# A forgetting-attention and SwiGLU kernel: loading q and k as eight rows per partition and moving the reordering to other reads of PSUM

## The chip, the cores and the metric

The kernel runs on one core of a Trainium2 chip. A core has a matrix engine (PE, in the profile also PEld for its weight loads), a vector engine (DVE), a scalar engine (ACT), a third elementwise engine (POOL) that does not touch PSUM in this kernel, and a queue engine (SP) that issues transfers; ACT and POOL issue a few transfers too. The metric is the device time of one execution in microseconds (us). Durations of single instructions are given in nanoseconds (ns).

## What is computed

There are 8 batches of 8 heads, 576 positions and a head size of 64. Each query row is scored against the keys up to its own position; a forget gate adds a decay that is a difference of cumulated log gates; a softmax and the weighted values follow. The result, 4608 tokens of 512 features, goes through a gated feed-forward block with 1536 hidden features.

```python
scores = scale * np.matmul(q, k.transpose(0, 1, 3, 2))
cum = np.cumsum(np.log(np.clip(f, 0.0001, 1.0)), axis=-1)
scores = np.where(causal, -1000000000.0, scores + cum[:, :, :, None] - cum[:, :, None, :])
attn = softmax(scores); x = np.matmul(attn, v)          # x: 4608 tokens x 512
g = x @ w_gate
out = (g * sigmoid(g) * (x @ w_val)) @ w_out
```

## The kernel before

The unit of the attention is a pair: two heads of one batch, 32 pairs in all (NPAIR). The 576 positions are cut into 9 blocks of 64 (QB), and a score tile holds 64 queries of one head in partitions 0 to 63 and the same 64 queries of the other head in partitions 64 to 127. The 9 query blocks of a pair are split into two groups, g=0 with blocks 0 to 3 and g=1 with blocks 4 to 8.

For one pair the steps are these. `load_pair` (L320) brings k and q in as float32, each with one transfer for both heads. Partition p holds a few consecutive rows: for k 96 partitions of 6 rows, for q 72 partitions of 8 rows (ROWS, L182). `prepare` (L337) casts them to bf16 (kb at L352, qb at L350, nearly always on POOL, on ACT at L348 for one pair of the start), transposes them on PE (L364) into a PSUM tile tx, 6 transposes of 96 columns for k and 8 of 72 for q, and copies tx to SBUF. The j-th transpose holds the rows j, j+6, j+12 and so on, so positions lie in tx in a permuted order. The copy (L380 on DVE, L378 on ACT) puts them back: it writes its target in natural order and reads PSUM with a step of 96 bf16 elements for k (tile kt, one copy for the pair) or 72 for q (tile qz, one copy for each head).

`scores` (L387) multiplies qz by kt into a PSUM tile sp (L399) and adds a causal mask to the last 64 columns of each query block with a second, 64-column matmul of the identity by the mask (L403). DVE then adds the gates' cumulated sum from cb, writes t, and keeps the running minimum (L415, a custom instruction); ACT takes the exponential (L429). `normalize` divides (L464 on POOL) into bf16 tiles pk. These are transposed, for the first 8 pairs on PE (L488, with copies at L493), for the others by a transposing transfer (L476), into pT. `weighted` (L496) multiplies by the values into xo, in the PSUM pool tx (L514), and `spread` (L521) copies the result into the ring xT (L538, ACT or DVE), the input of the feed-forward part. There `gate` makes two products (L595), tanh on ACT (L601, tile th, three buffers) and two DVE steps (L603, L606), and `project` (L609) makes the output product (L620), a copy and a transfer.

The order of everything is computed when the kernel is built. A planner (`Plan.order`, L54) holds for every step the engines that may do it with a cost for each, its dependencies, the buffer pools, and a priority; it always starts the step that can start first, ties by priority, and thereby also chooses the engine where several are allowed. Each engine then executes its own list in order. So a step's assumed cost, such as 600 on ACT and 680 on DVE for the copies of L378 and L380, decides both where it runs and what stands before and behind it. Feed-forward steps fill PE wherever attention steps cannot go; after the last attention step the rest of the feed-forward work follows.

Of the kernel before, what the change touches and what calls it, by code (L numbers as in the profile page):

```python
# [157 lines left out]
def kernel(  # L158
# [20 lines left out]
    NPAIR = B * NPB  # L179
    KD = DM // P  # L180
    KF = DF // P
    ROWS = {"k": (96, 6), "q": (72, 8)}  # L182
    scale = 1.0 / (D ** 0.5)
    assert NB * QB == S and D == 64 and all(a * b == S for a, b in ROWS.values())

    TILES = [256, 256] + [512] * 7 + [256, 256]
    NRING = 2560
# [34 lines left out]


    ident = sb.tile([P, P], BF16)
    maskf = sb.tile([P, QB], F32)
    mask = sb.tile([P, QB], BF16)
    xT = sb.tile([P, KD, NRING], BF16)
# [2 lines left out]
    wo = sb.tile([P, KF, DM], BF16)  # L230


    bufs("qf", [P, 2, ROWS["q"][1] * D], F32, 2)
    bufs("kf", [P, 2, ROWS["k"][1] * D], F32, 2)
    bufs("qb", [P, ROWS["q"][1], 2, D], BF16, 2)
    bufs("kb", [P, ROWS["k"][1], 2, D], BF16, 2)
    bufs("kt", [P, S], BF16, 5)
    bufs("qz", [P, NB, 2, QB], BF16, 5)
    bufs("cb", [P, S], F32, 5)
# [80 lines left out]
    def load_pair(p):  # L320
        b, hp = divmod(p, NPB)
        s = first[p]
        for name, src, pr in (("k", k, 0), ("q", q, .1)):
            pl.key((name + "f", p), name + "f")
            loads[name, p] = pl.op({"SP": 620} if p else {"ACT": 620}, lambda e, name=name, src=src: (nc.scalar if e == "ACT" else nc.sync).dma_start(
                out=pl.buf((name + "f", p))[0:ROWS[name][0], :, :],
                in_=src[b, 2 * hp:2 * hp + 2].rearrange("h (p r) d -> p h (r d)", r=ROWS[name][1])),
                (), [(name + "f", p)], (-99 + 3 * p if p < NPB else s) + pr, dma=1130 if name == "k" else 980, after=[sums[p - 3, 0 if p - 3 >= NPB else 1]] if p >= NPB else [])
        if p >= NDIRECT:
            pl.key(("cb", p), "cb")  # L330
            for h in range(2):
                loads["cb", p, h] = pl.op({"SP": 600}, lambda e, h=h: nc.sync.dma_start(
                    out=pl.buf(("cb", p))[64 * h:64 * h + 64, :],
                    in_=cum_dram[2 * p + h:2 * p + h + 1, :].to_broadcast((64, S))),
                    ["cum_dram"], [("cb", p), (("cb", p), 3)], -98.5 + 3 * p if p < NPB else s + .2, dma=560)

    def prepare(p):  # L337
        s = first[p]
        for name in ("k", "q"):
            fk, bk = (name + "f", p), (name + "b", p)  # L340
            KR, KC = ROWS[name]
            pl.key(bk, name + "b")

            def cast(e, name=name, fk=fk, bk=bk, KR=KR):
                src = pl.buf(fk)[0:KR, :, :].rearrange("p h (r d) -> p r h d", d=D)
                dst = pl.buf(bk)[0:KR, :, :, :]
                if e == "ACT":
                    nc.scalar.activation(dst, src, AF.Copy, scale=-scale if name == "q" else 1.0)  # L348
                elif name == "q":
                    eng[e].tensor_scalar(dst, src, -scale, 1.0, op0=ALU.mult, op1=ALU.mult)  # L350
                else:
                    eng[e].tensor_copy(dst, src)  # L352
            engs = {"POOL": 850}
            if p < NPB:
                engs = {"POOL": 850, "ACT": 850, "DVE": 500} if name == "k" else {"POOL": 1050, "ACT": 1050, "DVE": 680}
# [5 lines left out]
            def transpose(e, bk=bk, tk=tk, KR=KR, KC=KC):  # L361
                src = pl.buf(bk).rearrange("p r h d -> p r (h d)")
                for j in range(KC):
                    nc.tensor.transpose(half(tk)[:, KR * j:KR * j + KR], src[0:KR, j, :], ident[0:KR, 0:KR])  # L364
            pl.op({"PE": KC * (KR / 2.4 + 2.5)}, transpose, [bk], [tk], s - 1, lat=200)
            halves = [(0, P, None)] if name == "k" else [(0, 64, 0), (64, 128, 1)]
            ok = ("kt", p) if name == "k" else ("qz", p)
            pl.key(ok, ok[0])
            for a, z, h in halves:
                def evac(e, a=a, z=z, h=h, tk=tk, ok=ok, KC=KC):  # L370
                    if h is None:
                        src = half(tk)[a:z, 0:S].rearrange("r (j p) -> r p j", j=KC)
                        dst = pl.buf(ok)[a:z, :].rearrange("r (p j) -> r p j", j=KC)
                    else:
                        src = half(tk)[a:z, 0:S].rearrange("r (j i p) -> r i p j", j=KC, i=NB)
                        dst = pl.buf(ok)[a:z, :, h, :].rearrange("r i (p j) -> r i p j", j=KC)
                    if e == "ACT":
                        nc.scalar.copy(dst, src)  # L378
                    else:
                        nc.vector.tensor_copy(dst, src)  # L380
                pl.op({"ACT": 600, "DVE": 680}, evac, [tk] + ([("z", "qz", p)] if h is not None and p < 5 else []), [ok], s - .9)

    def epool(i):
        return f"e{i}" if i % 2 == 0 else "eo"
# [1 line left out]
    def scores(p, g):  # L386
# [3 lines left out]
        for n, bank in enumerate(BANKS[g]):  # L390
# [4 lines left out]
            def mult(e, bank=bank, sk=sk):  # L395
                sp, kt, qz, o = pl.buf(sk), pl.buf(("kt", p)), pl.buf(("qz", p)), 0
                for i, a, z in bank:
                    last = z == QB * (i + 1)
                    nc.tensor.matmul(sp[:, o:o + z - a], qz[:, i, :, :].rearrange("p h r -> p (h r)"), kt[:, a:z],  # L399
                                     start=True, stop=not last)  # L400
                    o += z - a
                    if last:
                        nc.tensor.matmul(sp[:, o - QB:o], ident, mask, start=False, stop=True)  # L403
            cols = [z - a for _, a, z in bank] + [64 for i, a, z in bank if z == QB * (i + 1)]
            pl.op({"PE": mm(*cols)}, mult, [("kt", p), ("qz", p), "mask"], [sk], pr, lat=220)
            o = 0
            for i, a, z in bank:
                last = z == QB * (i + 1)
# [4 lines left out]
                def add(e, i=i, a=a, z=z, o=o, sk=sk, tk=tk, last=last):  # L413
                    tm = pl.buf(("tm", p, g))
                    nc.vector.tensor_tensor_reduce(  # L415
                        out=pl.buf(tk)[:, a:z], in0=pl.buf(sk)[:, o:o + z - a], in1=pl.buf(("cb", p))[:, a:z], scale=1.0,
                        scalar=HUGE if a == 0 else tm[:, NB:NB + 1], op0=ALU.add, op1=ALU.min,
                        accum_out=tm[:, i:i + 1] if last else tm[:, NB:NB + 1])
                w = [tk, ("tm", p, g)] + ([("m", p, i)] if last else [("m", p, i, "part")])
# [101 lines left out]
    def spread(p, g):  # L521
# [5 lines left out]
        for a, z in ((0, cut), (cut, w)):  # L527
            if a == z:
                continue

            def evac(e, a=a, z=z):
                x0 = (t0 + a * QB) % NRING
                dst = xT[:, hp, x0:x0 + QB * (z - a)].rearrange("p (i r) -> p i r", r=QB)
                x = w - z
                src = pl.buf(xk)[:, QB * x:QB * (x + z - a)].rearrange("p (i r) -> p i r", r=QB)
# [183 lines left out]
```

## Time and profile before

| | |
|---|---|
| median of 3 runs | 437.74 us (436.67 to 437.89) |
| profiled execution | 437.73 us |
| its span, first to last instruction | 436.0 us |
| what lies around the span | 1.73 us |
| granted PE clock | 1.000 |
| busy PE / DVE / ACT / POOL | 402.5 / 347.9 / 302.8 / 252.1 us |
| instructions of PE / DVE / ACT / POOL | 3192 / 1081 / 848 / 452 |

All durations come from the profiled execution. The page lists busy time by engine, the span in 40 slices, the transfer queues, a chain of waits followed back from the last instruction, and the costliest groups of instructions. A group names its line, engine, operation, "output<-inputs", shapes and count, then busy time and mean, then the idle time of its engine before it and what ended that. PE's matmuls overlap in the pipeline: the duration of one (for example 379 ns for 512 columns) is its latency, and the distance between starts is what it occupies. "DMA share" can exceed 1 because transfers in flight overlap.

### The profile page before, as it was taken

The numbers are of one execution on the slowest core, as the hardware profiler recorded it, in microseconds if no ns is written. First come the engines' busy times: TensorE is split into PE (matmuls) and PEld (weight loads), VectorE is DVE, ScalarE is ACT, GpSimd is POOL, SyncE is SP. The second block draws the span as 40 slices with busy tenths as digits, with TensorE's granted clock in tenths as the row PEclk, the third lists the DMA queues.
The fourth block names the chain that finished last, engine by engine and source line by source line (L and its number), as shares of the span: only waits on it lengthen the run. The fifth ranks groups of instructions, "written<-read, shape, count | busy, mean of one in ns | idle before, by whom it ended". The sixth has DMA issues, their size and how long they took to land.

```text
span 436.0 us, 9859 instructions
## 1 busy us (share of the span) xinstructions
PE 402.5 (92%) x3192; PEld 229.2 (53%) x3192; DVE 347.9 (80%) x1081; ACT 302.8 (69%) x848; POOL 252.1 (58%) x452
## 2 busy tenths in 40 slices
PE   2578999998999998989999999999999999999996
PEld 1436777755454454444555554555445444457662
DVE  6788799798999798977999998999989665365340
ACT  6799789989877968776798777677678633232321
POOL 5699748748956855886668768938875600000000
PEclk9999999999999999999999999999999999999999
DMA  7999999637978998999999999999994640010112
GB/s 195 212 188 227 203 207 215 165 101 212 192 169 187 225 215 188 194 218 234 198 207 213 222 219 206 189 223 207 202 199 100 117 108 26 24 50 24 50 50 72
DMA packets 143956, 72.51 MB, mean 166 GB/s; under 512 B 118560, under 2 KB 130592, under 8 KB 143904
## 3 DMA queue, kind: packets, MB, share of 16 engines
q1 hardware_dynamic: 137732, 66.57, 71.9%
q0 software_dynamic: 5808, 4.72, 7.1%
q10 hardware_dynamic: 364, 0.59, 0.6%
q8 instruction: 25, 0.41, 0.4%
q14 instruction: 27, 0.22, 0.2%
HBM read 47.33 MB, written 9.58 MB: 131 GB/s over the span
## 4 chain that ended last, share of the span: by engine, by line
PE 60%; DVE 12%; DMA 10%; ACT 9%; POOL 4%; issue 4%; SPq 1%; DVEq 0%; ACTq 0%; POOLq 0%
PE gv L595 29%; PE op L620 15%; DMA qf<-in_q_dram 7%; PE sp L399 5%; DVE t L415 4%; PE tx L514 4%; ACT eo L429 3%; ACT e L429 2%; PE tx L364 2%; DVE qz L380 2%; DVE th L603 2%; POOL pk L464 2%; DMA pT<-pk 2%; PE gv L620 2%; DVE hh L606 2%
## 5 line engine op out<-in xcount | busy, mean ns | idle before, releaser
L415 DVE CUSTOM_DVE_ANT_0 t<-sp,cb 128x512 f32<-128x512 f32 (+7 forms) x288 | 130.4, 476 | 12.2 <-PE sp L403 5.9
L464 POOL TENSOR_SCALAR pk<-e,lr 128x512 bf16<-128x512 f32 (+3 forms) x186 | 97.7, 529 | 33.3 <-DVE tm L415 17.6
L595 PE MATMUL gv<-xT,wv 128*128 128x512 bf16 (+1 forms) x528 | 111.2, 340 | 0.2 <-DVE th L603 0.2
L595 PE MATMUL gv<-xT,wg 128*128 128x512 bf16 (+1 forms) x528 | 111.2, 340 | 0.2
L601 ACT ACTIVATE th<-gv 128x512 f32<-128x512 f32 x108 | 64.1, 594 | 61.0 <-PE gv L595 59.7
L603 DVE SCALAR_TENSOR_TENSOR th<-th,gv 128x512 f32<-128x512 f32 x108 | 73.9, 684 | 37.5 <-ACT th L601 37.1
L429 ACT ACTIVATE e<-t,tm 128x448 f32<-128x448 f32 (+4 forms) x160 | 88.8, 556 | 20.2 <-DVE tm L415 19.6
L620 PE MATMUL op<-wo,hh 128*128 128x512 bf16 x396 | 100.7, 379 | 2.1 <-DVE ot L632 1.3
L606 DVE TENSOR_TENSOR hh<-th,gv 128x512 bf16<-128x512 f32 x108 | 73.4, 685 | 10.3 <-PE op L620 4.1
L399 PE MATMUL sp<-kt,qz 128*128 128x448 bf16 (+4 forms) x320 | 72.3, 294 | 9.2 <-DVE tm L415 8.1
L429 ACT ACTIVATE eo<-t,tm 128x256 f32<-128x256 f32 (+3 forms) x128 | 71.2, 556 | 6.4 <-DVE tm L415 6.0
L595 PEld LDWEIGHTS <-wg 128*128 128x128 bf16 x528 | 48.9, 98 | 37.1 <-issue 0.2
L464 POOL TENSOR_SCALAR pk<-eo,lr 128x128 bf16<-128x128 f32 (+3 forms) x123 | 65.3, 531 | 2.5 <-ACT th L601 1.0
L595 PEld LDWEIGHTS <-wv 128*128 128x128 bf16 x528 | 47.8, 98 | 34.9 <-issue 0.3
L620 PEld LDWEIGHTS <-hh 128*128 128x128 bf16 x432 | 39.6, 98 | 41.8 <-issue 2.3
L403 PE MATMUL sp<-mask,ident 128*128 128x64 bf16 x288 | 48.1, 197 | 0.0
L399 PEld LDWEIGHTS <-qz 128*128 128x128 bf16 x320 | 30.6, 100 | 24.5 <-DVE qz L380 2.7
L350 POOL TENSOR_SCALAR qb<-qf 72x1024 bf16<-72x1024 f32 x31 | 32.9, 1062 | 14.8 <-DMA qf<-in_q_dram 7.2
L352 POOL CAST kb<-kf 96x768 bf16<-96x768 f32 x31 | 25.4, 820 | 27.4 <-DMA kf<-in_k_dram 19.3
L403 PEld LDWEIGHTS <-ident 128*128 128x128 bf16 x288 | 27.0, 100 | 21.3 <-issue 11.0
L557 POOL CAST vt<-vf 128x512 bf16<-128x512 f32 (+1 forms) x40 | 24.3, 608 | 17.4 <-DMA vf<-in_v_dram 17.2
L514 PE MATMUL tx<-pT,vt 128*64 128x320 bf16 (+4 forms) x448 | 29.7, 266 | 1.5 <-ACT e L429 0.5
(61 smaller groups left out, 393.2 us busy)
## 6 DMA issues: line engine op xcount, KB each, us to landing
out_dram<-ot SPq DMA_DIRECT2D x35, 256.0 KB, 2.4
kf<-in_k_dram SPq DMA_DIRECT2D x31, 288.0 KB, 6.3
qf<-in_q_dram SPq DMA_DIRECT2D x31, 288.0 KB
cb<-cum_f SPq DMA_DIRECT2D x62, 144.0 KB, 4.7
vf<-in_v_dram SPq DMA_DIRECT2D x32, 256.0 KB, 4.4
wo<-in_moe_w_out_dram POOLq DMA_DIRECT2D x3, 512.0 KB, 9.9
vf<-in_v_dram SPq DMA_DIRECT2D x8, 128.0 KB
wg<-in_moe_w_gate_dram POOLq DMA_DIRECT2D x2, 512.0 KB, 9.1
```

Source lines behind the costliest of these rows:

```text
L350: eng[e].tensor_scalar(dst, src, -scale, 1.0, op0=ALU.mult, op1=ALU.mult)
L399: nc.tensor.matmul(sp[:, o:o + z - a], qz[:, i, :, :].rearrange("p h r -> p (h r)"), kt[:, a:z], start=True, stop=not last)
L403: nc.tensor.matmul(sp[:, o - QB:o], ident, mask, start=False, stop=True)
L415: nc.vector.tensor_tensor_reduce(out=pl.buf(tk)[:, a:z], in0=pl.buf(sk)[:, o:o + z - a], in1=pl.buf(("cb", p))[:, a:z], scale=1.0, scalar= ...
L429: nc.scalar.activation(pl.buf(ek)[:, :L], pl.buf(tk)[:, :L], AF.Exp, bias=pl.buf(("tm", p, g))[:, i:i + 1], scale=-1.0, accum_out=pl.buf(( ...
L464: eng[e].tensor_scalar(dst, src, r, 1.0, op0=ALU.mult, op1=ALU.mult)
L514: nc.tensor.matmul(xo[r, 0:QB * n], vt[:, c, 2 * hp + h, :], pT[:, a:a + n, 64 * h:64 * h + 64], start=(c == 0), stop=(c == nch - 1))
L595: nc.tensor.matmul(pl.buf(bk)[:, j * n:j * n + n], wt[:, ko, fc * P:fc * P + P], xT[:, ko, x0:x0 + n], start=ko == 0, stop=ko == KD - 1)
L601: pl.op({"ACT": 487}, lambda e, u=u: nc.scalar.activation(pl.buf(("th", t, u)), pl.buf(("wg", t, u)), AF.Tanh, scale=0.5), [("wg", t, u)], ...
L603: pl.op({"DVE": 605}, lambda e, u=u: nc.vector.scalar_tensor_tensor(pl.buf(("th", t, u)), pl.buf(("th", t, u)), 1.0, pl.buf(("wg", t, u)), ...
L606: pl.op({"DVE": 605}, lambda e, u=u: nc.vector.tensor_mul(pl.buf(("hh", t, u)), pl.buf(("th", t, u)), pl.buf(("wv", t, u))), [("u", t, u), ...
L620: nc.tensor.matmul(pl.buf(bk), hh[:, (fc % nf) * n + ms * P:(fc % nf) * n + ms * P + P], wo[:, fc, :], start=fc == 0, stop=fc == KF - 1)
```

## The change

Both q and k now come in as 72 partitions of 8 rows (R = 8, PR = 72), so k has 8 transposes of 72 columns. The copies from PSUM no longer put anything in order for k: the copy of kt is a plain copy of 576 elements. For q the copy writes block by block, 64 columns a block, and reads PSUM in runs of 8 elements. Keys and queries therefore stay in a permuted order, and it is undone in two later places that read PSUM anyway. The score matmul reads kt in 8 runs of one eighth of its columns; the gate step reads sp with a step (an eighth of the matmul's columns, in float32) and writes t in natural key order. The queries stay permuted within each block of 64 until `spread`, whose copy reads the PSUM tile with a step of 8 within a block. The mask is made for that order of queries, and its matmul uses a permuted identity, perm, as the stationary operand and writes its 64 columns as 8 runs of 8. POOL makes perm once at the start. The planner's costs change: kb may cost 1050 instead of 850, a copy on DVE 380 instead of 680, and the transfer of q 1130 instead of 980. The tile th gets two buffers instead of three.

```diff
-    ROWS = {"k": (96, 6), "q": (72, 8)}
+    R = 8
+    PR = S // R
...
-    bufs("th", [P, 512], F32, 3)
+    bufs("th", [P, 512], F32, 2)
...
-            compare_op=ALU.is_ge, fill=BIG, base=0, pattern=[[-1, QB]], channel_multiplier=1,
+            compare_op=ALU.is_ge, fill=BIG, base=0, pattern=[[-1, R], [-R, R]], channel_multiplier=1,
...
+    setup({"POOL": 250}, lambda e: nc.gpsimd.tensor_copy(perm.rearrange("k (h j p) -> k h j p", h=2, j=R),
+                                                         ident.rearrange("k (h p j) -> k h j p", h=2, j=R)), ["perm"], -149)
...
-                out=pl.buf((name + "f", p))[0:ROWS[name][0], :, :],
-                in_=src[b, 2 * hp:2 * hp + 2].rearrange("h (p r) d -> p h (r d)", r=ROWS[name][1])),
+                out=pl.buf((name + "f", p))[0:PR, :, :],
+                in_=src[b, 2 * hp:2 * hp + 2].rearrange("h (p r) d -> p h (r d)", r=R)),
...
-            engs = {"POOL": 850}
+            engs = {"POOL": 1050}
...
-                for j in range(KC):
-                    nc.tensor.transpose(half(tk)[:, KR * j:KR * j + KR], src[0:KR, j, :], ident[0:KR, 0:KR])
+                for j in range(R):
+                    nc.tensor.transpose(half(tk)[:, PR * j:PR * j + PR], src[0:PR, j, :], ident[0:PR, 0:PR])
...
+                    src = half(tk)[a:z, 0:S]
                     if h is None:
-                        src = half(tk)[a:z, 0:S].rearrange("r (j p) -> r p j", j=KC)
-                        dst = pl.buf(ok)[a:z, :].rearrange("r (p j) -> r p j", j=KC)
+                        dst = pl.buf(ok)[a:z, :]
                     else:
-                        src = half(tk)[a:z, 0:S].rearrange("r (j i p) -> r i p j", j=KC, i=NB)
-                        dst = pl.buf(ok)[a:z, :, h, :].rearrange("r i (p j) -> r i p j", j=KC)
+                        src = src.rearrange("r (j i p) -> r i j p", j=R, p=R)
+                        dst = pl.buf(ok)[a:z, :, h, :].rearrange("r i (j p) -> r i j p", j=R)
...
-                pl.op({"ACT": 600, "DVE": 680}, evac, ...
+                pl.op({"ACT": 600, "DVE": 380}, evac, ...
...
-                    nc.tensor.matmul(sp[:, o:o + z - a], qz[:, i, :, :].rearrange("p h r -> p (h r)"), kt[:, a:z],
-                                     start=True, stop=not last)
+                    to = sp[:, o:o + z - a].rearrange("r (j p) -> r j p", j=R)
+                    nc.tensor.matmul(to, qz[:, i, :, :].rearrange("p h r -> p (h r)"),
+                                     kt.rearrange("d (j p) -> d j p", j=R)[:, :, a // R:z // R], start=True, stop=not last)
...
-                        nc.tensor.matmul(sp[:, o - QB:o], ident, mask, start=False, stop=True)
+                        nc.tensor.matmul(to[:, :, (z - a - QB) // R:], perm, mask.rearrange("r (j p) -> r j p", j=R),
+                                         start=False, stop=True)
...
-                        out=pl.buf(tk)[:, a:z], in0=pl.buf(sk)[:, o:o + z - a], in1=pl.buf(("cb", p))[:, a:z], scale=1.0,
+                        out=pl.buf(tk)[:, a:z].rearrange("r (p j) -> r p j", j=R),
+                        in0=pl.buf(sk)[:, o:o + z - a].rearrange("r (j p) -> r p j", j=R),
+                        in1=pl.buf(("cb", p))[:, a:z].rearrange("r (p j) -> r p j", j=R), scale=1.0,
...
-                src = bass.AP(src.tensor, src.offset + QB * (z - a - 1), [full[0], [-QB, z - a], full[2]])
+                src = bass.AP(src.tensor, src.offset + QB * (z - a - 1), [full[0], [-QB, z - a], [1, R], [R, R]])
```

More of the change, by code (lines that the diff above doesn't have):

```diff
@@ L181 @@
     KF = DF // P
-    ROWS = {"k": (96, 6), "q": (72, 8)}
+    R = 8
+    PR = S // R
     scale = 1.0 / (D ** 0.5)
-    assert NB * QB == S and D == 64 and all(a * b == S for a, b in ROWS.values())
+    assert NB * QB == S and D == 64 and R * R == QB
     TILES = [256, 256] + [512] * 7 + [256, 256]
@@ L224 @@
     ident = sb.tile([P, P], BF16)
+    perm = sb.tile([P, P], BF16)
     maskf = sb.tile([P, QB], F32)
@@ L230 @@
     wo = sb.tile([P, KF, DM], BF16)
[L233 to L236, printed above, removed]
+    bufs("qf", [P, 2, R * D], F32, 2)
+    bufs("kf", [P, 2, R * D], F32, 2)
+    bufs("qb", [P, R, 2, D], BF16, 2)
+    bufs("kb", [P, R, 2, D], BF16, 2)
     bufs("kt", [P, S], BF16, 5)
@@ L325, in load_pair @@
             loads[name, p] = pl.op({"SP": 620} if p else {"ACT": 620}, lambda e, name=name, src=src: (nc.scalar if e == "ACT" else nc.sync).dma_start(
[L326 to L328 removed]
+                out=pl.buf((name + "f", p))[0:PR, :, :],
+                in_=src[b, 2 * hp:2 * hp + 2].rearrange("h (p r) d -> p h (r d)", r=R)),
+                (), [(name + "f", p)], (-99 + 3 * p if p < NPB else s) + pr, dma=1130, after=[sums[p - 3, 0 if p - 3 >= NPB else 1]] if p >= NPB else [])
         if p >= NDIRECT:
@@ L352, in cast @@
                     eng[e].tensor_copy(dst, src)
-            engs = {"POOL": 850}
+            engs = {"POOL": 1050}
             if p < NPB:
-                engs = {"POOL": 850, "ACT": 850, "DVE": 500} if name == "k" else {"POOL": 1050, "ACT": 1050, "DVE": 680}
+                engs = {"POOL": 1050, "ACT": 1050, "DVE": 680}
             o = pl.op(engs, cast, [fk], [bk], s - 1 + (name == "q") * .1)
@@ L380, in evac @@
                         nc.vector.tensor_copy(dst, src)
-                pl.op({"ACT": 600, "DVE": 680}, evac, [tk] + ([("z", "qz", p)] if h is not None and p < 5 else []), [ok], s - .9)
+                pl.op({"ACT": 600, "DVE": 380}, evac, [tk] + ([("z", "qz", p)] if h is not None and p < 5 else []), [ok], s - .9)
     def epool(i):
@@ L398, in mult @@
                     last = z == QB * (i + 1)
-                    nc.tensor.matmul(sp[:, o:o + z - a], qz[:, i, :, :].rearrange("p h r -> p (h r)"), kt[:, a:z],
-                                     start=True, stop=not last)
+                    to = sp[:, o:o + z - a].rearrange("r (j p) -> r j p", j=R)
+                    nc.tensor.matmul(to, qz[:, i, :, :].rearrange("p h r -> p (h r)"),
+                                     kt.rearrange("d (j p) -> d j p", j=R)[:, :, a // R:z // R], start=True, stop=not last)
                     o += z - a
                     if last:
-                        nc.tensor.matmul(sp[:, o - QB:o], ident, mask, start=False, stop=True)
+                        nc.tensor.matmul(to[:, :, (z - a - QB) // R:], perm, mask.rearrange("r (j p) -> r j p", j=R),
+                                         start=False, stop=True)
             cols = [z - a for _, a, z in bank] + [64 for i, a, z in bank if z == QB * (i + 1)]
-            pl.op({"PE": mm(*cols)}, mult, [("kt", p), ("qz", p), "mask"], [sk], pr, lat=220)
+            pl.op({"PE": mm(*cols)}, mult, [("kt", p), ("qz", p), "mask", "perm"], [sk], pr, lat=220)
             o = 0
```

17 lines of the change are left out of this document (8 added, 9 removed).

## The prediction

> **What bounds the kernel now.** I read the page's busy times first, then busy time by stage, then the chain of waits, then the groups with shapes kept apart.
>
> ```profile
> PE 402.5 (92%) x3192; PEld 229.2 (53%) x3192; DVE 347.9 (80%) x1081; ACT 302.8 (69%) x848; POOL 252.1 (58%) x452
> ```
>
> By stage (start-up, attention with feed-forward filling, feed-forward alone):
>
> ```profile
> core 0: us, PE busy (x) PEld busy (x) DVE busy (x) ACT busy (x) POOL busy (x), PEclk, DMA share, GB/s
> 0.00:40.00 40.00, 22.51 (x213) 15.31 (x214) 31.49 (x114) 32.56 (x93) 30.86 (x71) 1.00 1.01 206
> 40.00:340.00 300.00, 288.16 (x2436) 162.75 (x2434) 271.29 (x890) 239.81 (x698) 216.17 (x372) 1.00 0.96 196
> 340.00:436.00 96.00, 91.83 (x547) 51.09 (x545) 45.09 (x79) 30.40 (x60) 5.11 (x10) 1.00 0.21 57
> ```
>
> PE is nearly full from 40 us on, and DVE is at 90% in the attention stage. A busy PE counts latencies, so I measured what a matmul occupies from the starts in the timeline:
>
> ```profile
> 205.74 0.28 PE L399 MATMUL sp<-kt,qz 128*128 128x256 bf16 x1
> 205.86 0.19 PE L403 MATMUL sp<-mask,ident 128*128 128x64 bf16 x1
> 205.89 0.25 PE L399 MATMUL sp<-kt,qz 128*128 128x192 bf16 x1
> ...
> 207.01 0.42 PE L364 MATMUL tx<-ident,kb 96*128 96x96 bf16 x6
> 207.26 0.42 PE L364 MATMUL tx<-ident,qb 72*128 72x72 bf16 x8
> 207.52 1.03 PE L595 MATMUL gv<-xT,wv 128*128 128x512 bf16 x4
> ```
>
> 256 columns take 0.12 us, 64 take 0.03, six transposes of 96 take 0.25 and eight of 72 take 0.26: columns / 2.4 + 2.5 ns, the same rule that gives 216 ns for 512 columns. Summed over all starts, PE has 379 us of such work. In the 432 us from the span's start to the end of the last matmul it lies empty 4.8 us before the first one, 22.2 us in the rest of the first 40, 25.6 us from 40 to 340 and 0.5 us later. Those 48 us between matmuls are all that a change without PE work in it can win. The chain says who owns them:
>
> ```profile
> PE 60%; DVE 12%; DMA 10%; ACT 9%; POOL 4%; issue 4%; SPq 1%; DVEq 0%; ACTq 0%; POOLq 0%
> PE gv L595 29%; PE op L620 15%; DMA qf<-in_q_dram 7%; PE sp L399 5%; DVE t L415 4%; PE tx L514 4%; ACT eo L429 3%; ACT e L429 2%; PE tx L364 2%; DVE qz L380 2%; DVE th L603 2%; POOL pk L464 2%; DMA pT<-pk 2%; PE gv L620 2%; DVE hh L606 2%
> ```
>
> The reader is to see DVE as second, with the copy of qz, which the change touches, among its lines.
>
> **Copies out of PSUM, on DVE.** These rows decide:
>
> ```profile
> L380 DVE COPY qz<-tx 64x576 bf16<-64x576 bf16 x36 | 27.2, 754 | 4.1 <-PE tx L364 1.8 <-ACT qz L378 1.5
> L380 DVE COPY kt<-tx 128x576 bf16<-128x576 bf16 x20 | 15.0, 752 | 2.0 <-PE tx L364 1.8
> L378 ACT COPY kt<-tx 128x576 bf16<-128x576 bf16 x12 | 7.6, 633 | 3.7 <-PE tx L364 3.7
> ...
> L493 DVE COPY pT<-gv 128x1024 bf16<-128x1024 bf16 x6 | 4.1, 688 | 1.0 <-PE gv L488 0.8
> L493 DVE COPY pT<-gv 128x384 bf16<-128x384 bf16 x4 | 1.4, 349 | 0.4 <-PE gv L488 0.4
> ```
>
> L493 copies bf16 from PSUM without a step at (688 - 349) / 640 = 0.53 ns per element, so 576 elements without a step cost 349 + 192 x 0.53 = 451 ns. With a step they cost 752 to 754, 1.04 ns per element. For kt I take 451. For qz, in runs of 8, the trace has no row: between 451 and 754; I take 451, since its neighbours in a run adjoin as in L493. ACT gains nothing: its row at 1024 elements is 1009 and at 384 it is 485, which gives 642 for 576, beside 633 measured with the step.
>
> The order of instructions shows 19 + 44 such copies on DVE (20 + 36 before), so DVE has 63 x 0.451 = 28.4 us instead of 42.2: 13.8 less. A few other copies move to it (+1.5), so 12.3 us less. ACT has 33 of them instead of 40 and a little less besides: 5.5 us less.
>
> What of it is on the path: adding up the chain's pieces, 12 of qz (8.9 us) and 4 of kt (2.8) stand in it on DVE. One such place:
>
> ```profile
> 45.74 0.44 PE tx L364 x6
> 46.21 0.77 DVE kt L380
> ```
>
> 40% of those 11.7 us is **4.7 us**. The lower bound is 2.7: kt's 1.2, and 0.125 for each of 12 qz pieces if the other head's copy on ACT (629) is then the last. The upper bound is 0.9 x 12.3 = 11.1, if every microsecond that leaves DVE were waited for while it is busy, 90% of the stage. I take 4.7: what is late next is PE's own work, which the chain shows 60% of the time.
>
> **PE.** k's eight transposes of 72 cost 0.26 us instead of 0.25: +0.3 us over 32 pairs. The PE lists hold the same work in almost the same interleaving: the last attention matmul has 303 us of PE work up to it instead of 304. Reading kt in runs of 8 to 64 elements: L514 reads in runs of 64 and takes 307 ns for 320 columns, where L399 takes 305 for 320 in one run; I take nothing. The 288 mask matmuls, 224 of them now written as 8 runs of 8: the trace has no stepped write. Lower bound 0, upper bound twice the 29 ns, 6.5 us; I take 0, the nearer row being L514's runs. perm loads like ident (100 ns, hidden).
>
> **Reads with a step of float32**, in L415 and L538. The copies of L380 and L378 skip 192 or 144 bytes at every element and take 1.04 ns per element on DVE and 0.82 on ACT, and L415 already takes 683 - 277 = 406 ns for 384 more elements, 1.06 each. A read that already goes element by element has no pairing to lose, and longer skips cost these rows nothing, which excludes a loss and a gain: 0.
>
> **POOL and the loads.** L352 takes 820 ns for 768 elements and L557 609 for 512, 0.82 each, so kb costs 1.03 instead of 0.82: 31 x 0.21 = 6.5 us. POOL is 72% busy in the attention stage and kb stands in the chain in 3 pieces, 2.4 us, of which a quarter more is **+0.6 us**, with bounds of 0 and 6.5. The 72-partition load is different in kind: the trace's landing records show 16 steps for each kf and 13 for each qf, which I read as 12 rings in use and one step for the other four. From the end of the issue to the last landing after 60 us kf takes 4.6 us and qf 4.9 on average. k now loads as q does: 0.3 us later per pair, hidden by the load ahead, except at the start, where loads of pairs 0 to 2 stand in front of a q that POOL waits for. There three loads with 12 packets of 87 ns per ring instead of 12 of 65 give **+0.8 us**. Elsewhere it costs up to 10 x 0.3 = 3.0, since POOL waited for kf 10 times. Start-up's ACT list is shorter by some copies, about 1.2 us; I count that as part of the DVE term's upper side, not again. SP's list keeps its transfers and nearly their order.
>
> **th with two buffers.** A tanh, 594, and two DVE steps, 684 and 685, make 1.96 us per tile. In the last stage PE brings one tile per about 2.6 us (280 us of feed-forward work over 108 tiles), and two buffers carry that. In the attention stage the planner's order already holds it: 0.
>
> **Sum.** -4.7 + 0.3 + 0.6 + 0.8 = -3.0 us, from the profiled execution's 437.73 (1.73 of them around the span): **434.7 us**, -0.7%. The median of the runs, 437.74, is the same to 0.01. A measurement here tells about 0.3%, 1.3 us, from no change.
>
> **Rivals.** (a) *The saved DVE time is hidden*: DVE's longest waits behind the copies end on PE (1.8 us), and only 3.4 us of PE's waits from 40 to 340 are put down to L415. Then only the lower bound, 2.7, meets the additions of 1.7: 436.7, no change. Against it: DVE is full to 90%.
> (b) *Loads and POOL take over*: POOL waited for kf 10 times, 19.3 us in all. If each of these 10 pairs is then late by 0.21 + 0.3 us on the path, that is +5.1, with 1.1 of PE and start-up, against the lower bound's -2.7: 441.2, slower. It is slower by more than 1.3 us from the sixth such pair on. For it: DMA share 0.96; against: PE's waits for POOL's qb and kb are 3.4 us from 40 to 340.
> (c) *The mask's stepped write halves PE's rate there*: +6.5 us at L403, on an engine that is full, with the rest of the sum 441.2, slower. It decides from 3.0 us / 224 = 13 ns a matmul. Against it: nothing in the trace steps a write, so only the floor of 29 ns speaks.
> (d) *The copy of qz stays at 754*: then DVE saves 20 x 752 - 19 x 451 - 8 x 754 = 0.4 us, the planner, assuming 380, puts 44 of them on DVE, and the chain gains 1.2 of kt less 1.7 of additions: 438.2, no change.
>
> The Trainium skill (PSUM: Partial Sum Buffer, Specifications) says that any pattern without adjoining elements slows matmuls significantly, with lines of 8 bytes; it gives no price, and no row here shows one. By that rule the time would be (c)'s 441.2 or more, against 434.7 by the rows; the written runs of 8 float32 hold four such lines each, so I read it as weak here.
>
> **Chances.** Forecast 0.54, (a) 0.17, (b) 0.11, (c) 0.09, (d) 0.09. The forecast's own range is 428.3 (11.1 in place of 4.7) to 436.4 (the 1.3 us limit). The range for 8 in 10 is 428.3 to 441.2: it takes in the forecast, (a) and (d), 0.80, and reaches to where (b) and (c) lie. Faster by over 0.3%: 0.53 (the forecast's, and a little of (a)); within: 0.24; slower: 0.23.
>
> **What would show it.** L380's kt and qz rows near 451 ns; L415 and L403 as before by shape (a mean start distance of 29 ns behind L403); kb at 1.03 us; 13 landings for kf; PE's empty time from 40 to 340 down from 25.6 to about 22. Wrong if L415's 512-column form leaves 683, if qz is at 754, or if the waits of PE for kb and qb grow past 3 us more.

## The result and the profile after

The changed kernel is slower: a median of 444.44 us (443.04 to 445.1, four runs) beside 437.81 us of the kernel before on the same chip. The medians differ by 6.6 us; the ratio is 1.0145, with an interval from 1.0118 to 1.0172, which is 6.3 us. Its profiled execution took 444.67 us, its span 442.9, which is 6.9 more than before. Some runs that another state of the chip disturbed are left out of every comparison here.

The page of the kernel after, busy times, then the chain of waits by engine and by line:

```profile
PE 404.6 (91%) x3256; PEld 231.5 (52%) x3256; DVE 336.1 (76%) x1089; ACT 296.6 (67%) x841; POOL 257.1 (58%) x452
...
PE 48%; DMA 17%; POOL 14%; issue 7%; DVE 6%; ACT 6%; SPq 2%; POOLq 0%; DVEq 0%; ACTq 0%
PE gv L605 24%; PE op L630 12%; POOL pk L474 10%; DMA qf<-in_q_dram 7%; DMA vf<-in_v_dram 6%; PE sp L406 4%; PE tx L524 3%; DVE t L423 3%; POOL qb L356 2%; ACT e L439 2%; PE tx L370 2%; DMA pT<-pk 2%; PE gv L630 2%; ACT eo L439 2%; DMA kf<-in_k_dram 1%
```

DVE gave up 11.8 us, as forecast (12.3), and its share of the chain fell from 12% to 6%. PE's share fell too, from 60% to 48%, and DMA and POOL rose together from 14% to 31%. So the work that left DVE was not replaced on the path by PE's work, which the prediction expected to be "late next", but by loads and by POOL. Most of POOL's share is the division that makes pk (10%, 2% before), and most of what the loads gained is v's (6%; before, it was not among the lines shown).

The groups of after, shapes kept apart (count, then busy time and mean ns of one, then the engine's idle time before it):

```profile
L423 DVE CUSTOM_DVE_ANT_0 t<-sp,cb 128x512 f32<-128x512 f32 x64 | 43.8, 684 | 6.2 <-PE sp L406 2.2 <-PE sp L410 1.5 <-ACT lr L453 0.9
L386 DVE COPY qz<-tx 64x576 bf16<-64x576 bf16 x44 | 19.9, 452 | 9.4 <-PE tx L370 5.9 <-ACT qz L384 2.0 <-ACT e L439 1.0
L386 DVE COPY kt<-tx 128x576 bf16<-128x576 bf16 x19 | 8.6, 452 | 3.7 <-PE tx L370 3.6
...
L358 POOL CAST kb<-kf 72x1024 bf16<-72x1024 f32 x31 | 32.0, 1033 | 28.9 <-DMA kf<-in_k_dram 28.9
```

The prices of the changed instructions came out as worked out: copies of 452 ns in runs of 8 too, the gate step at 684 ns beside 683, the cast of k at 1033. What is new stands in the last column of the cast: POOL waited 28.9 us for k's loads. The waits of POOL in after, first for v and then for k (us in total, times, longest), and below them the same two rows of before:

```profile
POOL vt L567 <- DMA vf<-in_v_dram: 30.1, 19, 3.5
POOL kb L358 <- DMA kf<-in_k_dram: 28.9, 11, 6.8
```

```profile
POOL kb L352 <- DMA kf<-in_k_dram: 19.3, 10, 6.6
POOL vt L557 <- DMA vf<-in_v_dram: 17.2, 17, 1.9
```

Together 36.5 us became 59.0. The load of v, which the change does not touch, is the one whose waits grew more. Those are waits of an engine with idle time; what counts is whether they reach PE. The waits of PE in after:

```profile
PE tx L370 <- POOL qb L356: 7.7, 10, 1.3
PE sp L406 <- DVE tm L423: 6.4, 15, 1.1
PE tx L370 <- ACT kb L354: 6.3, 1, 6.3
PE op L630 <- ACT ot L640: 3.2, 3, 1.8
PE tx L370 <- POOL kb L358: 2.9, 5, 1.2
```

and of before:

```profile
PE sp L399 <- DVE tm L415: 8.1, 18, 1.7
PE tx L364 <- ACT kb L348: 4.8, 1, 4.8
PE tx L364 <- POOL qb L350: 4.7, 6, 1.5
...
PE tx L364 <- POOL kb L352: 1.0, 2, 0.5
```

PE's waits for DVE's gate step fell by 1.7 us, which is what the change won in these rows. Its waits for POOL's two casts rose from 5.7 to 10.6 us, those for the first cast of k by 1.5, and those for a copy of the output product on ACT from 0.2 to 3.2. From the starts of PE's matmuls, each counted with what one of its size occupies at the full clock: PE's work is the same (379.4 us beside 379.3), and the empty time before the first matmul went from 4.8 to 6.3 us, in the rest of the first 40 us from 22.2 to 22.9, from 40 to 340 us from 25.6 to 28.4, and behind that from 0.5 to 2.5. The four increases add up to 7 us, and the spans differ by 6.9: all of the loss is time in which PE does not get on.

The start is plain. In after:

```profile
5.19 1.06 ACT L354 ACTIVATE kb<-kf 72x1024 bf16<-72x1024 f32 x1 [1.96 <-DMA kf<-in_k_dram]
```

and in before:

```profile
3.90 0.84 ACT L348 ACTIVATE kb<-kf 96x768 bf16<-96x768 f32 x1 [0.53 <-DMA kf<-in_k_dram]
```

The first cast begins 1.29 us later, because k's load lands later, and takes 0.22 us longer.

Not all of the empty time is waiting. The granted PE clock is 0.66 from 36 to 41 us in after and 1.00 in before, and the count of empty time takes in what a matmul occupies longer at a lower clock. Nineteen transposes of pk show it, first in after, then in before:

```profile
38.22 2.21 PE L498 MATMUL gv<-ident,pk 128*128 128x128 bf16 x19
35.90 1.50 PE L488 MATMUL gv<-ident,pk 128*128 128x128 bf16 x19
```

Directly, at most (1 - 0.66) x 5 = 1.7 us of this execution can be due to that. No run sets the clock by itself, so its part in the 6.6 us stays open.

Landings, measured from the end of the issue to the last landing step, mean of the loads issued after 60 us: k 4.64 before and 5.12 after, q 4.93 and 5.51, v 4.14 and 4.75, cb 3.58 and 3.73. The loads of k now land in 13 steps instead of 16, which the prediction read as 12 engines' steps and one for the other four. The Trainium skill (DMA: Bandwidth & Descriptors, Why a DMA increments its semaphore by 16 and not by 1) says that a load is split over the largest number of engines up to 16 that divides its outermost dimension; 72 rows give 12, 96 give 16. The trace agrees: 13 steps for 72 partitions, 16 for 96. I call these engines rings, as the prediction does. What a load over fewer of them costs is asked of the experiments.

### The profile page after: what moved, and what is told of

It is laid out like the page before. It is cut to its first block, busy times and chain, and to the rows that moved or that the text cites. A ratio compares the mean times of both kernels' runs of the same rounds, so it can differ in the third digit from the quotient of the medians.

```text
span 442.9 us, 9986 instructions
## 1 busy us (share of the span) xinstructions
PE 404.6 (91%) x3256; PEld 231.5 (52%) x3256; DVE 336.1 (76%) x1089; ACT 296.6 (67%) x841; POOL 257.1 (58%) x452
## 4 chain that ended last, share of the span: by engine, by line
PE 48%; DMA 17%; POOL 14%; issue 7%; DVE 6%; ACT 6%; SPq 2%; POOLq 0%; DVEq 0%; ACTq 0%
PE gv L605 24%; PE op L630 12%; POOL pk L474 10%; DMA qf<-in_q_dram 7%; DMA vf<-in_v_dram 6%; PE sp L406 4%; PE tx L524 3%; DVE t L423 3%; POOL qb L356 2%; ACT e L439 2%; PE tx L370 2%; DMA pT<-pk 2%; PE gv L630 2%; ACT eo L439 2%; DMA kf<-in_k_dram 1%
## 5 line engine op out<-in xcount | busy, mean ns | idle before, releaser
L439 ACT ACTIVATE e<-t,tm 128x448 f32<-128x448 f32 (+4 forms) x160 | 88.5, 554 | 22.2 <-DVE tm L423 22.1
L474 POOL TENSOR_SCALAR pk<-eo,lr 128x512 bf16<-128x512 f32 (+3 forms) x122 | 64.6, 530 | 3.3 <-DVE lr L457 2.9
L358 POOL CAST kb<-kf 72x1024 bf16<-72x1024 f32 x31 | 32.0, 1033 | 28.9 <-DMA kf<-in_k_dram 28.9
L410 PE MATMUL sp<-mask,perm 128*128 128x64 bf16 x288 | 48.1, 198 | 0.0
L406 PEld LDWEIGHTS <-qz 128*128 128x128 bf16 x320 | 31.4, 101 | 24.9 <-DVE qz L386 2.8
L567 POOL CAST vt<-vf 128x512 bf16<-128x512 f32 (+1 forms) x40 | 24.3, 609 | 34.0 <-DMA vf<-in_v_dram 30.1
L410 PEld LDWEIGHTS <-perm 128*128 128x128 bf16 x288 | 27.3, 101 | 19.7 <-issue 9.5
```

The lines of the kernel that those rows point to most:

```text
L406: nc.tensor.matmul(to, qz[:, i, :, :].rearrange("p h r -> p (h r)"), kt.rearrange("d (j p) -> d j p", j=R)[:, :, a // R:z // R], start=Tru ...
L410: nc.tensor.matmul(to[:, :, (z - a - QB) // R:], perm, mask.rearrange("r (j p) -> r j p", j=R), start=False, stop=True)
L439: nc.scalar.activation(pl.buf(ek)[:, :L], pl.buf(tk)[:, :L], AF.Exp, bias=pl.buf(("tm", p, g))[:, i:i + 1], scale=-1.0, accum_out=pl.buf(( ...
L474: eng[e].tensor_scalar(dst, src, r, 1.0, op0=ALU.mult, op1=ALU.mult)
```

## The experiments

The theories were: (1) the load of k, now over 12 rings, is what costs, by landing later and making others land later; (2) POOL's longer cast costs; (3) the planner's new costs give a worse order; (4) th with two buffers costs; (5) the copies win nothing or the stepped accesses cost. The expectations call the first four L, P, O and T. All ratios are to the kernel before, run on the same chip; e1 to e4, e5 to e8, e9 to e12 and e13 to e16 each had a chip of their own, so a comparison between these groups takes it that a ratio carries over from chip to chip. "q's landing" is the mean defined above (for e1_split the mean over both parts of a load, each from the end of its own issue), and "POOL for v" the total wait of POOL for the loads of v. e7_order_load left no trace that can be compared.

| run | ratio (95%) | q's landing, us | POOL for v, us |
|---|---|---|---|
| before | 1 | 4.93 | 17.2 |
| after | 1.0145 (1.0118 to 1.0172) | 5.51 | 30.1 |
| e1_split | 1.0234 (1.0187 to 1.0281) | 4.23 | 30.9 |
| e2_before_k72 | 1.0200 (1.0167 to 1.0234) | 5.52 | 31.4 |
| e3_before_th2 | 1.0013 (0.9982 to 1.0044) | 4.87 | 25.2 |
| e4_q_alone | 1.0010 (0.9986 to 1.0034) | 5.15 | 22.1 |
| e5_order | 1.0027 (0.9996 to 1.0058) | 5.14 | 23.0 |
| e6_order_pool | 1.0069 (1.0039 to 1.0098) | 5.37 | 20.4 |
| e7_order_load | 1.0144 (1.0089 to 1.0200) | | |
| e8_after_order2 | 1.0163 (1.0112 to 1.0215) | 5.71 | 32.8 |
| e9_k80 | 1.0195 (1.0137 to 1.0253) | 5.49 | 22.1 |
| e10_after_80 | 1.0031 (1.0000 to 1.0063) | 5.01 | 22.6 |
| e11_before_q80 | 1.0032 (1.0004 to 1.0059) | 4.85 | 24.1 |
| e12_q_alone_q80 | 1.0033 (1.0008 to 1.0058) | 5.24 | 23.7 |
| e13_after_k80 | 1.0128 (1.0075 to 1.0181) | 5.64 | 23.6 |
| e14_after_q80 | 1.0182 (1.0147 to 1.0217) | 5.56 | 23.9 |
| e15_k72_both80 | 1.0121 (1.0091 to 1.0152) | 5.35 | 24.4 |
| e16_after_start80 | 1.0146 (1.0110 to 1.0182) | 5.49 | 28.5 |
| e17_after_early | 1.0102 (1.0037 to 1.0167) | 5.47 | 30.3 |
| e18_before_early | 0.9974 (0.9935 to 1.0013) | 5.20 | 22.1 |

### The parts one at a time

**e1_split**: after, with each load of q and k as two transfers, of 64 and of 8 partitions.

```diff
+                for x, y in ((0, 64), (64, PR)):
+                    (nc.scalar if e == "ACT" else nc.sync).dma_start(
+                        out=pl.buf((name + "f", p))[x:y, :, :],
```

> The changed kernel, with each load of k and q issued as two transfers, 64 partitions and 8 partitions, and nothing else changed. Theory L (a load of 72 partitions uses 12 rings and leaves 4 idle; with k on them too the loads land later, POOL and PE wait): all 16 rings carry work, kf and qf land as early as kf did before (4.6 us after the issue instead of 5.1 and 5.5), the first matmul starts at about 5 us instead of 6.3, and the time is 434 to 438 us. Theory T (two th buffers) and theory O (the planner's new order fits the chip worse): the time stays at 443 to 446.

The landings did come earlier (k 3.99, q 4.23, v 3.87 us), yet the kernel became slower still, and the 434 to 438 us that theory L expected of that did not come. The start shows a new cost, here the issues and PE's first matmul:

```profile
0.74 1.74 ACTq L334 DMA_DIRECT2D kf<-in_k_dram  x2
...
2.52 2.53 ACTq L334 DMA_DIRECT2D qf<-in_q_dram  x2
...
7.58 0.66 PE L373 MATMUL tx<-ident,kb 72*128 72x72 bf16 x8 [7.58 <-ACT kb L357]
```

A pair of issues keeps ACT's queue busy for 1.7 to 2.5 us where one took 0.3 to 0.7, and PE starts at 7.6 us instead of 6.3. Since earlier landings were bought with longer issues, the run neither shows nor refutes the theory of the load.

**e2_before_k72**: before, with k alone loaded in 72 partitions of 8 rows, the planner's costs for that, and th in two buffers. The copies keep their step. Three of its edits:

```diff
-    ROWS = {"k": (96, 6), "q": (72, 8)}
+    ROWS = {"k": (72, 8), "q": (72, 8)}
...
-    bufs("th", [P, 512], F32, 3)
+    bufs("th", [P, 512], F32, 2)
...
-            engs = {"POOL": 850}
+            engs = {"POOL": 1050}
```

> The kernel before with only k's load, cast and transposes taken from the change: 72 partitions of 8 rows, the planner's costs for them, and two th buffers; copies with a step and everything behind them as before. Theory L: it has the whole damage and none of the gain, 446 to 449 us, kf landing at 5.0 us or later. Theory T: about 444, as much as two th buffers alone. Theory O (the damage comes with the copies' new cost of 380): 437 to 439.

k landed 4.88 us after its issue, a little under the 5.0 named. This part alone costs 2.0%, more than the whole change. So the loss comes with k's 8 rows (their load, their cast, the order planned for them, th), and not with the new places of the reordering.

**e3_before_th2**: before, with two buffers of th.

```diff
-    bufs("th", [P, 512], F32, 3)
+    bufs("th", [P, 512], F32, 2)
```

> The kernel before with two th buffers instead of three, nothing else. Theory L: 437.5 to 439. Theory T: 443 to 445, with PE's empty time behind 340 us grown from 0.5 to 2 us or more.

No time that can be told from nothing (+0.6 us, interval -0.8 to 1.9), although PE's empty time behind 340 us goes from 0.5 to 2.3 us, as in after. So of after's four increases the last one, 2.0 us, comes with th; whether it costs that much of the whole time, this interval can't tell.

**e4_q_alone**: before, with only q's half of the change (its copy in runs of 8, the permuted mask and identity, the read in the copy of x, the planner's 380 for q's copy); k's load, transposes and copy as before, th with three buffers. One of its edits:

```diff
-                        src = half(tk)[a:z, 0:S].rearrange("r (j i p) -> r i p j", j=KC, i=NB)
+                        src = half(tk)[a:z, 0:S].rearrange("r (j i p) -> r i j p", j=KC, i=NB)
```

> The half of the change that concerns q: queries stay permuted up to the copy of x, the mask goes through perm, q's copies read runs and cost 380 in the plan; k as before (96 partitions of 6 rows, copy with a step, natural key order, mask written in one run), three th buffers. Theory L: the gain of q's faster copies without the load's price, 433 to 436 us. Theory O: 441 to 445, since the new cost of 380 is what changes the order. Theory T: 433 to 436 too.

```profile
L387 DVE COPY qz<-tx 64x576 bf16<-64x576 bf16 x37 | 16.7, 453 | 5.6 <-PE tx L371 2.9 <-ACT qz L385 2.2
L387 DVE COPY kt<-tx 128x576 bf16<-128x576 bf16 x16 | 12.0, 750 | 1.5 <-PE tx L371 1.3
```

The copies of qz run at 453 ns and DVE has 338.9 us of work, 9.0 less than before, and the time is the same: 1.0010. None of the three ranges named for it holds the 439.6 us measured. In this order at least, less work on DVE brought the end no nearer. PE's empty time from 40 to 340 us was 27.6 us, not less than 25.6.

### The same order, one price at a time

The planner's costs change the order of instructions in e2 and in after. The four kernels that follow have exactly e2's order: they differ from it, and from each other, only in what an instruction does.

**e5_order**: before's instructions, with th in two buffers and the planner told of e2's costs. One of its edits:

```diff
-            pl.op({"PE": KC * (KR / 2.4 + 2.5)}, transpose, [bk], [tk], s - 1, lat=200)
+            pl.op({"PE": 8 * (72 / 2.4 + 2.5)}, transpose, [bk], [tk], s - 1, lat=200)
```

> The instructions of the kernel before (k in 96 partitions, th with two buffers), executed in exactly the order that the planner made for e2, the kernel before with k in 72 partitions: only the plan's costs are e2's. Theory O (the order made from the new costs fits the chip worse): 1.5 to 2% slower than before, as e2 was. Theories L (the load of k in 72 partitions) and P (POOL's longer cast): within 0.4% of before.

**e6_order_pool**: e5 with one more small copy on POOL behind each cast of k, into a tile that nobody reads.

```diff
+                    if e == "POOL":
+                        nc.gpsimd.tensor_copy(idle[0:KR, 0:KX], pl.buf(fk)[0:KR, 0, 0:KX])
```

> As e5, with one more POOL instruction behind each cast of k, a copy of 32 elements of kf to a spare tile, about 0.21 us, the time by which the cast of 72 partitions is longer; same order. Theory P: 1 to 2% slower than before. Theories O and L: as e5 to within 0.4%.

The added copy takes what k's longer cast takes (1033 - 820 = 213 ns):

```profile
L356 POOL CAST idle<-kf 96x32 bf16<-96x32 f32 x31 | 6.4, 207 | 0.0
```

**e7_order_load**: e2 with a cast of only 6 of k's 8 rows (820 ns instead of 1033). It leaves out two rows of each partition, so a quarter of the keys are zeros.

```diff
+                n = 6 if name == "k" else KC
```

> e2 with the cast of k shortened to what it cost before: it converts 6 of the 8 rows of a partition and leaves out the other two (the two stay zero, so part of the keys count as zero). Load and transposes are e2's, and so is the order. Theory L: 1.5 to 2% slower than before, kf landing like qf. Theory P: within 0.5% of before. Theory O: as e5.

**e8_after_order2**: after, with the planner's old cost of a copy on DVE, which gives e2's order.

```diff
-                pl.op({"ACT": 600, "DVE": 380}, evac, ...
+                pl.op({"ACT": 600, "DVE": 680}, evac, ...
```

> The changed kernel with 680 instead of 380 as the plan's cost of a copy on DVE, which gives it e2's order to the instruction. Against e2 only the copies are faster (452 instead of 752 ns) and the stepped reads and writes of the change are in. If the copies are on the path as the chain suggested, 4 to 5 us under e2, 1.0 to 1.2% over before; if they are hidden, like e2, 1.8 to 2.2% over before. If the new reads and writes of PSUM cost anything, more than e2.

The steps from before to after are then quotients of the ratios in the table; the intervals add the half widths in quadrature, and 1% is 4.38 us.

| step | from, to | change, % | us |
|---|---|---|---|
| order and th | before, e5 | +0.27 (-0.04 to 0.58) | 1.2 |
| POOL's longer cast | e5, e6 | +0.42 (-0.01 to 0.85) | 1.8 |
| k's load in 72 partitions | e6, e2 | +1.30 (0.86 to 1.74) | 5.7 |
| copies and stepped accesses | e2, e8 | -0.36 (-0.97 to 0.25) | -1.6 |
| the new order with DVE at 380 | e8, after | -0.18 (-0.76 to 0.40) | -0.8 |

The load stands out: the only step whose interval is clear of zero, and e7 gives nearly the same with both runs on one chip (e5 to e7: +1.17, 0.53 to 1.81). It includes the eight transposes of 72 for six of 96, 0.3 us. In this order PE's waits for POOL's two casts are 4.9 us in e5, 2.6 in e6 and 9.3 in e2, and the wait for the first cast 4.8, 4.9 and 5.9; the traces of e5 and e6 lack some records of matmuls, so these figures are rough.

### Is it the 12 rings?

Each of these kernels loads 80 partitions where 72 are needed (the last 8 hold rows of the next head or pair that nobody reads), so that 16 rings take part. The bytes grow by a ninth. The last pair keeps 72.

```diff
+    def rows80(p):
+        return 80 if p < NPAIR - 1 else 72
+
+    def view80(x, n):
+        return bass.AP(x.tensor, x.offset, [[8 * D, n], [S * D, 2], [1, 8 * D]])
...
+                out=pl.buf((name + "f", p))[0:rows80(p), :, :], in_=view80(src[b, 2 * hp:2 * hp + 2], rows80(p))),
```

**e9_k80**: e2, with k in 80.

> e2 with one thing changed: each load of k brings 80 partitions instead of 72 in one transfer (8 partitions of rows of the next head, which nothing reads; the last pair keeps 72). 80 is divisible by 16, so by theory R (what costs in the load is that 72 partitions go over 12 rings) all 16 steps of landing appear for kf, and the load's price of 1.2% is gone although a tenth more bytes move: 0.5 to 0.9% over before, like e6. Theory S (the cost lies in the shape itself, 2048-byte rows and fewer partitions, or in the start): 1.7 to 2.3% over before, like e2.

**e10_after_80**: after, with k and q in 80.

> The changed kernel with 80 partitions in each load of k and of q, in one transfer each (the last pair keeps 72). Theory R: both loads get 16 rings, q's for the first time; 0.5% under to 0.5% over before. Theory S: 1.2 to 1.9% over before, like the changed kernel.

**e11_before_q80**: before, with q in 80 (k has 96).

> The kernel before with only q's load widened to 80 partitions (the last pair keeps 72). Theory R: q's load gets 16 rings and lands about 0.3 us earlier; 0.3 to 1.0% under before, so that the kernel before too had a loss there. Theory S: within 0.3% of before or a little over, for the tenth more of bytes.

**e12_q_alone_q80**: e4, with q in 80.

> e4 (q's half of the change alone) with q's load widened to 80 partitions. Theory R: under e4 by 0.3 to 1.0%, so 0.2 to 0.9% under before. Theory S: as e4, within 0.3% of before.

**e13_after_k80** and **e14_after_q80**: after, with only k, or only q, in 80.

> The changed kernel with 80 partitions in k's load only, q's stays at 72. Of the four cases with the changed kernel's order, k and q at 72 measured 1.0145 and both at 80 measured 1.0031. If rings count and act transfer by transfer, this one lies halfway, 1.006 to 1.011. If what counts is only that no load of the pair is confined to 12 rings, it stays at 1.012 to 1.018, as e9 did in e2's order.

> The changed kernel with 80 partitions in q's load only, k's stays at 72. Transfer by transfer: 1.006 to 1.011. All or nothing: 1.012 to 1.018. If q's load, the last of a pair to land, is the one that counts: 1.002 to 1.006.

**e15_k72_both80**: e2, with k and q in 80.

> e2 with 80 partitions in both loads. If rings are the load's price in e2's order as well, it falls from 1.020 to e6's level, 1.005 to 1.010. If e10's gain belongs to the changed kernel's order alone, it stays at 1.015 to 1.022.

**e16_after_start80**: after, with k and q in 80 for the first four pairs only.

> The changed kernel with 80 partitions in both loads of the first four pairs only; the other 28 pairs keep 72. If the price of the 12 rings is paid at the start, where nothing stands ahead of the loads, most of e10's gain is here: 1.002 to 1.007. If it is paid in every pair: 1.011 to 1.015.

In after's order, 16 rings for both loads take back 1.1% (1.0031 beside 1.0145), more bytes notwithstanding, and e10 differs from after in nothing but these loads. In e2's order both take back 0.8% (e15 beside e2). Only one of them takes back nothing that the intervals can tell (e9, e13, e14), and the start alone nothing (e16), though PE then begins at 5.5 us instead of 6.3. Where k has 96 partitions, 16 rings for q gain nothing (e11 beside before, e12 beside e4).

So the number of rings of k's load is not its price by itself. In e6 and in e9 k goes over 16 rings and q over 12, in the same order, and e9 is 1.25% slower (0.60 to 1.90). What differs is the shape, 80 partitions of 8 rows for 96 of 6, with a ninth more bytes for k and 0.3 us more of transposes. e15, with 16 rings for both loads, still lies 0.5% (0.1 to 0.9) over e6.

The waits of POOL in e10:

```profile
POOL kb L363 <- DMA kf<-in_k_dram: 24.0, 10, 7.1
POOL vt L572 <- DMA vf<-in_v_dram: 22.6, 15, 3.6
```

Both waits are shorter than in after (28.9 and 30.1), and PE, DVE and ACT stand in the chain of waits nearly as in before (e10's trace too lacks some records of matmuls):

```profile
PE 58%; DVE 13%; ACT 10%; POOL 7%; issue 6%; DMA 4%; SPq 1%; DVEq 0%; POOLq 0%; ACTq 0%
```

These waits do not tell the time, though: e13 has 20.1 us for k and 23.6 for v, and is 1.0% slower than e10; e2 has only 8.5 for k. Nor does the granted clock explain what e10 took back: its mean over the runs is 0.992 in e10 and 0.993 in after.

Over the kernels with one transfer per load, the ratio goes with q's landing: up to 5.24 us in those at 1.0033 or less, 5.35 and 5.37 in e15 and e6, and 5.47 or more in all others that have a trace, which are at 1.010 or above. That is a correlation; the mean landing was not set by itself in any run.

What stays open: q in 72 beside k in 96 costs nothing (e11), and q in 72 beside k in 80 as much as both in 72 (e13), with k landing as late (5.12 us in both). The number of rings of each load alone doesn't say that; the 12-ring loads of a pair and the following load of v in one queue would have to be followed ring by ring, which these traces don't give.

### Loading earlier

**e17_after_early** and **e18_before_early**: after and before, where the loads of a pair wait for the sums of the pair four before it instead of three.

```diff
-... after=[sums[p - 3, 0 if p - 3 >= NPB else 1]] if p >= NPB else [])
+... after=[sums[p - 4, 0 if p - 4 >= NPB else 1]] if p >= NPB else [])
```

> The changed kernel with the loads of k and q allowed one pair earlier: each waits for the exponentials of four pairs before instead of three; 72 partitions in both. Theory N (the price is paid because a load lands after its cast could start): the lateness gets cover, and the time falls to 1.000 to 1.008 of before with less of PE's empty time ahead of the transposes. Theory V (the price is paid by whatever queues behind the loads on the rings, the loads of v and cb among it): no better than 1.012, and more waits for vf.

> The control: the kernel before with the same earlier loads. Theory N: its loads are mostly in time, 0.995 to 1.002. Theory V: the same or slower, 1.000 to 1.008.

After gains 0.4% and before 0.3%, both within their intervals. PE's waits for POOL's casts fall to 4.0 us in e17, below before's 5.7, and the kernel is still at 1.0102. So PE's waits for a pair's own casts are not the whole of it: POOL's wait for v stays at 30.3 us, and the order of the loads in the queue has changed with it. Where the rest is lost isn't settled. No version here is clearly faster than before.

## Why the prediction was wrong

- **The load of k** is the step that failed. It said that k "now loads as q does: 0.3 us later per pair, hidden by the load ahead, except at the start", +0.8 us, and "Elsewhere it costs up to 10 x 0.3 = 3.0". Measured: +1.30% of 438, 5.7 us. In the step from e6 to e2, 1.0 us of it lies ahead of the first matmul (4.9 and 5.9 us; 1.5 from before to after), so most of it falls later, where the prediction took it to be hidden. The 0.3 us itself, read from q's 4.9 beside k's 4.6, was near: k landed 0.48 later in after, and 0.12 from e6 to e2. What the step left out is the other loads, which are made as before: in after q landed 0.58 us later and v 0.61, where the order has changed too; in one order, from e6 to e2, q landed 0.15 later and v 0.38 (4.02 and 4.40). The wait for v, in no term of the sum, grew by 12.9 us on POOL, the one for k by 9.6, and POOL's list has casts of k and q behind those of v. By which of these the load of k takes its 5.7 us isn't shown: POOL's waits do not go with the time, and 12 rings instead of 16 are not enough, since k in 80 partitions, over 16 rings, cost about as much (e9, e13) and only both loads in 80 took most of it back.
- **The copies** were forecast at -4.7 us. The sizes of the copies were right, and also DVE's saving (11.8 of 12.3). The saving on the path was -1.6 us in the same order (interval -4.2 to 1.1) and nothing in e4. The rule "40% of the pieces on the chain" failed: a chain names one path, and the chain of after suggests that POOL's work and the loads were only a little behind DVE's. Rival (a), 2.7 us, was nearer.
- **POOL's cast** was forecast at +0.6 with an upper bound of 6.5; the measured 1.8 us has an interval from 0 to 3.7.
- **The order** was taken to cost nothing because PE's list had kept its interleaving. Order and th together are +1.2 us (-0.2 to 2.5) in e2's order; the order with the cheap copies is 0.8 us better than that one, within its interval of nothing.
- **Rival (b)**, loads and POOL take over, came nearest: the loss does come with k's load and, less surely, POOL's longer cast, 7.5 us in the two steps where it had 5.1. Its time, 441.2 us, was too low beside 444.4; it counted ten waits for k at 0.5 us each and none for v. A DMA share of 0.96 and 36.5 us of POOL's waits for two loads spoke for a chance above 0.11.
- **Rival (c)**, the mask's stepped write, is refuted: L410 takes 198 ns (197 before), and the median distance of starts behind a mask matmul is 29 ns in both. The Trainium skill (PSUM — Partial Sum Buffer, Specifications (TRN2)) says that any non-contiguous pattern slows matmuls significantly. These runs of 8 float32 don't bear that out.
- **Rival (d)**, a copy of qz that stays at 754 ns, is refuted by 452.
- **The marks** named: kt and qz at 451, L415 and L403 as before, kb at 1.03 us and 13 landings all came true. PE's empty time from 40 to 340 us went up to 28.4 instead of down to 22, and the waits of PE for kb and qb in that stretch, named as what would make it wrong, grew from 3.4 to 7.9 us.

## What to carry to other kernels

When a change alters the shape of a transfer, price the loads beside it too: here two loads that the change leaves alone landed 0.6 us later, and the wait for one of them grew most. A count of rings foretold e10 and failed in e9, e11 and e12, so run also the cases that a count says will gain. Time taken off an engine that is 90% busy in a stage is worth what a run shows, not its share of the chain; here 9 to 12 us less of DVE's work gave 0 to 1.6 us. To tell a planner's order from the work itself, build kernels that keep one order and change one price.

## What the runs showed of the hardware

- DVE copies bf16 from PSUM at the same 452 ns per 576 elements whether the read adjoins throughout (kt) or in runs of 8 (qz); with a step at each element it takes 752.
- The gate step reads float32 from PSUM with a step of up to 64 elements at no cost: 684 beside 683 ns for 512.
- PE writes 64 columns to PSUM as 8 runs of 8 at the same 29 ns per matmul as in one run.
- Loading 80 partitions where 72 are needed, a ninth more bytes, made the landings shorter: q 5.51 to 5.01 us and k 5.12 to 4.60 when both were widened in after's order. With k alone widened they stayed at 5.64 and 5.12.
- Splitting a load in two costs issue time on the queue's engine: 1.7 to 2.5 us per pair of issues in the start, where one issue took 0.3 to 0.7.
